# Attention and a gated FFN on one core: the last visits dealt anew, a step in halves in single banks, and X's transpositions no longer held

## The chip, the cores and the metric

The kernel runs on one core of a Trainium2 chip. The metric is device time in microseconds (us). Times before: a median of 419.72 us over three runs (419.26 to 419.96).

## The reference

```python
# q, k, v: (8, 12, 448, 64); w_gate, w_val: (768, 1536); w_out: (1536, 768)
scores = (q @ k.transpose(0, 1, 3, 2)) / sqrt(64)
attn = exp(scores - scores.max(-1)); attn = attn / attn.sum(-1)
x = (attn @ v).transpose(0, 2, 1, 3).reshape(8 * 448, 12 * 64)
g = x @ w_gate
out = (g * sigmoid(g) * (x @ w_val)) @ w_out          # (3584, 768), float32
```

Softmax attention over 8 batches and 12 heads is followed by a gated feed-forward network (FFN) over all 3584 tokens.

## The kernel before

The work is one hand-written order of instructions; the framework adds the waits, and each engine goes through its own list in order.

**Attention** goes by pairs of heads, 48 of them (6 in each batch). For a pair the queries and keys are copied by GpSimd (L240) and turned by a DMA transposition that SyncE (SP) issues (L244, tile `qkT`). TensorE makes scores `s` (L356, and L368 for leftover keys of two pairs together), ScalarE takes the exponential into `E` (L378), TensorE multiplies by V (L462, tile `acc`), and VectorE divides (L504, L505) into `xt`. `turn_x` turns `xt` into the matrix `X`, by DMA transpositions on SP: one of a pair's 384 long tokens (L550), and after each odd pair one of the 64 short tokens of two pairs (L556). `xt` has six buffers, so a pair reuses the buffer of the pair six before it. `X` holds two batches; the tiles come from a pool of two.

**The FFN of the first two X matrices** is done in between. A block has 384 or 512 tokens and 12 steps, one for each 128 columns of the hidden layer. A step makes a gate (`gp`, L610) and a value (`vp`, L610), each of six accumulating matmuls; ScalarE takes a tanh (`sg`), VectorE combines it with the gate (`t1`) and closes with the value (L696, into `hts`). It is run in one of three ways: whole (`run_fv`), as a pair of two steps (`run_pair`, 512 tokens wide, with the second step's value in halves), or in halves (`halves`, L660): gate halves of 256 tokens, two tanh (L670), two combinations (L675), two value halves, two closings (L696). A hidden block is then multiplied by `w_out`: by groups (`OutPair.wide`, L807, seven-product scheme, matmuls on L759), and, for the chunk of 128 tokens left over, by quarters of 192 columns (`plain_out`, L724, 12 matmuls on L732), scaled into `osb` by ScalarE (L742) or VectorE (L740); the fourth quarter also issues the chunk's two output DMAs.

**PSUM** is handed out by two pools: `ps_s`, three tiles of two banks, and `ps_f`, two single banks. Scores take `ps_s`, the products `acc` two of `ps_f`. A new tile waits for the readers of the tile three (or two) before it in its pool. `gate_small` tells a step to put its gate into `ps_f`; it is set in visits without products. `halves` doesn't look at it before the change.

**Visits.** The stretch around the change is a list of 33 visits (`VISITS`, L1108), each with up to three score tiles, up to one pair's products, and what its entry says: (block to begin, steps, groups, quarters, sums of VectorE). Every seventh visit is bare: it has scores but no products. They are the visits numbered 3, 10, 17, 24 and 31 from 0. In visit 24 the entry asks for two steps, which are run as a pair. A visit with one step and products runs it in halves (`lone`, L1297). Quarters stand in visits 25, 26, 27 and 29, groups in 28 and 31. `by_vector` (L1391) puts the scaling of the quarters on VectorE, except in visit 26. In the last visits, pairs 36 to 41 and on belong to the last X, whose buffer is that of the second X; as long as steps of the second X are left, their `turn_x` is held (`held`, L1345) and run after the last step (L1412).

After the visits come two phases of `Unit` (L929 onwards) and `OutPair` work for the last two X matrices, with sums of weights on GpSimd and sums of tokens on VectorE.

Of the kernel before, what the change touches and what calls it, by code (L numbers as in the profile page):

```python
# [10 lines left out]
FP32 = mybir.dt.float32  # L11
FP16 = mybir.dt.float16
# [5 lines left out]
NB = 2  # L18
# [10 lines left out]
NX = 6  # L29
# [36 lines left out]
def kernel(  # L66
# [10 lines left out]
    nc = tc.nc  # L77
    B, H, S, D = q.shape
# [4 lines left out]
    NCB = DM // 128  # L83
    NFB = DF // 128
    NHP = H // 2
# [5 lines left out]
    MQ = S - D  # L91
    KR = MQ // 128
# [18 lines left out]
    xp = ctx.enter_context(tc.tile_pool(name="xp", bufs=2))  # L111
# [10 lines left out]
    xts = consts.tile([128, NX, 8, D], FP16, name="xt")  # L122
# [35 lines left out]

    raw = {}
    qkT = {}  # L160
    X = {}

    def dummy(n, w=4):
        wp = ps_f.tile([128, 512], FP32, tag="f", name="wp")
# [362 lines left out]
        for c in range(NC):  # L527
            pv_chunk(pr, c)

    def turn_x(pr):  # L530
        b, hp = divmod(pr, NHP)
        kk, bb = divmod(b, NB)
        if kk not in X:
            X[kk] = xp.tile([128, NCB, NB * S], FP16, tag="X", name="X")
        dst = X[kk][:, hp, ts(bb, S)]
        xt = Xts[pr % NX]
        if pr < XPE:
            tp = accs[pr] if pr < FIRST else ps_f.tile([128, 512], FP32, tag="f", name="xtp")
            for j in range(3):
                nc.tensor.matmul(  # L540
                    tp[:, ts(j, 128)],
                    lhsT=xt[:, 2 * j : 2 * j + 2].rearrange("p h d -> p (h d)"),
                    rhs=ident[:],
                    start=True,
                    stop=True,
                )
            nc.vector.tensor_copy(dst[:, 0:MQ], tp[:, 0:MQ])
            return
        odd = pr % 2
        nc.sync.dma_start_transpose(  # L550
            dst[:, 0:MQ].rearrange("p (j q) -> p j q", j=KR),
            xt[:, 2 * odd : 2 * (KR + odd)].rearrange("p j d -> p (j d)"),
        )
        if odd:
            flat = xts[0:D, ts(pr % NX // 2, 2)].rearrange("p a j d -> p (a j d)")
            nc.sync.dma_start_transpose(X[kk][:, hp - 1 : hp + 1, ds(bb * S + MQ, D)], flat[:, ds(2 * KR * D, 4 * D)])  # L556

    def turn_rests(b):
        if b == 0:
# [15 lines left out]
    gate_small = [False]  # L575
# [23 lines left out]
    class Step:  # L599
# [60 lines left out]
        def halves(self):  # L660
            w = self.at[2] // 2
            parts = [ds(i * w, w) for i in range(2)]
            gs = ps_s.tile([128, 2, 512], FP32, tag="s", name="gp")
            self.sg = fp.tile([128, 512], FP32, tag="sg", name="sg")
            self.t1 = fp.tile([128, 512], FP32, tag="t1", name="t1")
            readers = []
            for i, part in enumerate(parts):
                g = gs[:, i, 0:w]
                apart(self.group("g", gs[:, i], range(NCB), (i * w, w)), *readers)
                tanh = nc.scalar.activation(self.sg[:, part], g, AF.Tanh, scale=0.5)  # L670
                for reader in readers[1:2]:
                    tc.declare_no_dep(tanh.ins, reader.ins, reason="another bank")
                readers.append(tanh)
                readers.append(
                    nc.vector.scalar_tensor_tensor(self.t1[:, part], self.sg[:, part], 1.0, g, ALU.add, ALU.mult)  # L675
                )
            while late_exp:
                late_exp.pop(0)()
            vps = [ps_f.tile([128, 512], FP32, tag="f", name="vp") for _ in parts]
            for i, vp in enumerate(vps):  # L680
                self.group("v", vp, range(NCB), (i * w, w))
            for i, vp in enumerate(vps):
                self.close(i * w, w, vp)
# [38 lines left out]
    by_vector = [False]  # L722
# [150 lines left out]
    NT = NB * S  # L873
# [152 lines left out]
    with tc.manual_schedule():  # L1026
# [52 lines left out]
        def add_block(i, visits):  # L1079
# [36 lines left out]
        ]  # L1116

        def token_sums(x, w, t, eng=nc.vector):
# [156 lines left out]
        base = min(x for x in adds if adds[x] == 2)  # L1275
        KL = B // NB - 1
        held = []
# [6 lines left out]
        for x, (chunks, todo) in enumerate(plan):  # L1284
# [9 lines left out]
            begins, nf, ng = VISITS[x - base][:3] if x >= base else (0, 0, 0)  # L1294
            if begins > 2:
                add_block(begins, 0)
            lone = nf == 1 and bool(todo)  # L1297
            behind = []
            for n, (pr, c) in enumerate(ordered if x else []):
                if ng and not todo:  # L1300
# [36 lines left out]
            for _, p0 in todo:  # L1337
                if split:
                    pv_split(p0)
                else:  # L1340
                    pv(p0)
                if p0 < XPE:
                    turns.append(p0)
                elif fvq and fvq[0].at[0] < p0 // NHP // NB - 1:
                    held.append(p0)  # L1345
                else:
                    turn_x(p0)
            for turn in ready:
# [9 lines left out]
            if 0 < base - x <= len(FIRST_STEPS):  # L1358
                n = FIRST_STEPS[x - base]
                gate_small[0] = bare  # L1360
                if n > 1:
                    run_pair()
                elif x < base - 1:
                    run_fv(True)
                    add_sum()
                else:
                    fvq.pop(0).halves()
                    add_sum()
            elif x < base:
                if bare and oq and not fvq:  # L1370
                    carry -= run_o()
                elif bare:
                    gate_small[0] = True
                out_small[0] = not fvq and bool(oq) and any(p0 >= QUAD for _, p0 in todo)
                extra = 2 * fvq[0].time if bare and len(chunks) == 3 and fvq and not fvq[0].at[1] else 0
                carry = run_budget(left() / (end - x) + carry + extra) - extra
            else:
                begins, nf, ng, no, ns = VISITS[x - base]
                gate_small[0] = bare
                out_small[0] = bool(no) and not bare  # L1380
                for _ in range(ng):
                    run_group(behind)
                if lone:
                    fvq.pop(0).halves()
                    add_sum()
                elif bare_next(x):
                    for _ in range(nf):
                        run_fv()
                else:
                    run_steps(nf)  # L1390
                by_vector[0] = x != len(VISITS) + base - 7  # L1391
                for _ in range(no):
                    run_o()
                    out_small[0] = True
                out_small[0] = False
                if begins == 2:
                    add_block(2, 0)
                ahead = {3: (x + 1, x + 2), 2: (), 1: ()}.get(len(VISITS) + base - x, (x + 1,))
                for p0 in [p for y in ahead for p in vcopies.get(y, [])]:
                    copy_v(p0)  # L1400
                add_sum(ns)
                if x == len(VISITS) + base - 6:
                    wsum_space(rfree[:, 2 * NK * S :], 3)
                    for t in qk16s:
                        wsum_space(t[:].rearrange("p t c h d -> p (t c h d)"), 2)
                    wsum_space(Eall, 4)
                    tsums6.extend(token_sums(X[KL - 1], S, t6))
# [2 lines left out]
            for u in {len(VISITS) + base - 6: range(2), len(VISITS) + base - 2: range(2, 3)}.get(x, []):  # L1410
                weight_sums(u)
            while held and not fvq:  # L1412
                turn_x(held.pop(0))
            while turns:
                turn_x(turns.pop(0))
        kept.extend(attp.tile([128, S], FP32, tag="qkT", name="kept", bufs=QB) for _ in range(4))
# [78 lines left out]
        p0 = NPAIR - 1  # L1495
# [13 lines left out]
        run_items(items)  # L1509

        apart_chunk = vfree[:, 6 * VE :].rearrange("p (f t) -> p f t", t=128)
        t7 = token_space(xp.tile([128, NCB, NT], FP16, tag="X", name="T")[:].rearrange("p a b -> p (a b)"), S)
        sums.clear()
        sums.extend(f for pair in pairs[1:] for f in pair.sums())
        sums.extend(token_sums(X[KL], S, t7))
# [41 lines left out]
```

## Time and profile before

| | |
|---|---|
| median of three runs | 419.72 us |
| profiled execution | 420.08 us |
| its span, first to last instruction | 418.3 us |
| granted TensorE clock in it | 1.000 |
| busy: PE / DVE / ACT / POOL | 412.2 / 273.7 / 248.9 / 225.4 us |
| visits 24 to 31 begin (us from the span's start) | 232.96, 238.95, 241.57, 244.40, 247.13, 255.75, 258.50, 260.17 |

In the profile PE is TensorE's matmuls, PEld its weight loads, DVE is VectorE, ACT ScalarE, POOL GpSimd, SPq the queue of SyncE. A timeline row gives start, duration, engine, line, operation, tiles and shapes; rows of equal instructions in a row are merged, with their count behind an x, and the duration is then from the first start to the last end. What an engine waited for stands in brackets. Matmuls are pipelined, so a matmul's row is longer than the spacing of starts.

### The profile page before, as it was taken

How to read it: one execution, taken by the hardware profiler on the slowest of the kernel's cores; microseconds unless marked ns; L12 is line 12 of the kernel's file. 1: busy time of each engine (PE TensorE's matmuls, PEld its weight loads, DVE VectorE, ACT ScalarE, POOL GpSimd, SP SyncE). 2: the span in 40 equal slices, each digit the busy share in tenths (PEclk: the TensorE clock that was granted, in tenths of full speed). 3: DMA queues.
4: the chain of work that ended last, by engine and by line, in shares of the span. 5: the costliest groups of instructions: out<-in, count | busy, mean ns of one | idle time of the engine just before them, and what ended most of it. 6: DMA issues, size and time to landing. Idle time of an engine off the chain costs nothing.

```text
span 418.3 us, 10870 instructions
## 1 busy us (share of the span) xinstructions
PE 412.2 (99%) x4346; PEld 260.4 (62%) x4346; DVE 273.7 (65%) x630; ACT 248.9 (59%) x387; POOL 225.4 (54%) x346
## 2 busy tenths in 40 slices
PE   8999999999999999999999999999999999999996
PEld 3666666655587786786767676555555655555664
DVE  4767562567786674579646578766757665757763
ACT  6975677656677675787656695655453345454121
POOL 8856534998898986398976814599800000000000
PEclk9999999999999999999999999999999999999999
DMA  9999999999999999999999935600000430000225
GB/s 135 192 200 200 200 177 195 129 166 205 196 142 179 153 194 172 154 158 151 167 159 171 102 62 106 186 18 0 2 0 2 121 107 0 2 0 0 76 79 150
DMA packets 108195, 50.29 MB, mean 120 GB/s; under 512 B 60400, under 2 KB 104816, under 8 KB 108144
## 3 DMA queue, kind: packets, MB, share of 16 engines
q0 software_dynamic: 46848, 24.56, 48.3%
q1 hardware_dynamic: 61024, 24.79, 34.7%
q8 instruction: 34, 0.56, 0.6%
q10 hardware_dynamic: 272, 0.25, 0.2%
q14 instruction: 17, 0.14, 0.1%
HBM read 49.55 MB, written 11.01 MB: 145 GB/s over the span
## 4 chain that ended last, share of the span: by engine, by line
PE 94%; DVE 2%; ACT 2%; issue 1%; ACTq 0%; DVEq 0%
PE gp L610 14%; PE un L929 12%; PE vp L610 12%; PE og L759 11%; PE ub L929 10%; PE ob L759 8%; PE acc L462 8%; PE s L356 5%; PE op L732 4%; PE s L393 2%; PE acc L426 2%; PE s L368 1%; PE tp L324 1%; PE wp L166 1%; ACT E L403 1%
## 5 line engine op out<-in xcount | busy, mean ns | idle before, releaser
L378 ACT ACTIVATE E<-s 128x896 f16<-128x896 f32 x126 | 107.4, 916 | 38.2 <-PE s L356 28.0
L610 PE MATMUL gp<-X,wg 128*128 128x256 f16 (+3 forms) x402 | 61.7, 300 | 0.0
L610 PE MATMUL vp<-X,wv 128*128 128x256 f16 (+3 forms) x402 | 58.6, 289 | 0.4 <-DVE xt L505 0.4
L240 POOL COPY qk<-qkraw 128x512 f16<-128x512 f16 x70 | 43.5, 668 | 22.8 <-DMA qkT<-qk 21.7
L180 POOL DMA_DIRECT2D vraw<-in_v_dram x72 | 44.1, 637 | 14.8 <-DMA wo<-in_moe_w_out_dram 8.0
L610 PEld LDWEIGHTS <-wv 128*128 128x128 f16 x444 | 41.6, 98 | 15.3 <-DVE xt L505 0.9
L610 PEld LDWEIGHTS <-wg 128*128 128x128 f16 x402 | 35.5, 98 | 15.8 <-issue 2.2
L180 POOL DMA_DIRECT2D qkraw<-in_k_dram x70 | 42.7, 630 | 4.9 <-DMA wo<-in_moe_w_out_dram 3.5
L403 ACT ACTIVATE E<-s 112x896 f16<-112x896 f32 x48 | 40.7, 918 | 7.5 <-PE s L393 7.5
L462 PEld LDWEIGHTS <-E 128*128 128x128 f16 (+2 forms) x1224 | 38.2, 98 | 8.5 <-issue 3.1
L462 PE MATMUL acc<-vo,E 128*128 128x65 f16 (+2 forms) x1224 | 42.1, 193 | 0.1
L759 PEld LDWEIGHTS <-hts 128*128 128x128 f16 x282 | 27.1, 98 | 17.0
L690 DVE SCALAR_TENSOR_TENSOR t<-sg,gp 128x384 f32<-128x384 f32 (+1 forms) x29 | 17.4, 614 | 24.3 <-ACT sg L637 24.3
L696 DVE SCALAR_TENSOR_TENSOR hts<-t,vp 128x256 f16<-128x256 f32 (+3 forms) x67 | 30.9, 461 | 3.5 <-PE vp L610 1.2
L505 DVE TENSOR_TENSOR xt<-acc,R 128x256 f16<-128x256 f32 x72 | 30.6, 425 | 2.5
L203 POOL DMA_DIRECT2D qkraw<-in_q_dram x44 | 30.2, 685 | 3.0 <-PE s L393 1.0
L356 PE MATMUL s<-qkT 64*64 64x448 f16 (+1 forms) x288 | 28.5, 352 | 0.0
L1002 ACT ACTIVATE silu<-un 128x448 f32<-128x448 f32 x24 | 13.1, 544 | 21.7 <-PE un L929 20.0
L759 PE MATMUL og<-wo,hts 128*128 128x384 f16 x132 | 25.4, 326 | 0.0
L986 DVE TENSOR_TENSOR un<-ub,kept 128x448 f32<-128x448 f32 x24 | 15.1, 631 | 15.6 <-ACT kept L983 10.2
L990 DVE TENSOR_TENSOR kept<-ub,kept 128x448 f32<-128x448 f32 x24 | 15.0, 625 | 13.2 <-PE ub L929 13.2
L979 ACT ACTIVATE ub<-un 128x448 f32<-128x448 f32 x24 | 12.7, 529 | 15.4 <-PE un L929 13.9
(213 smaller groups left out, 748.2 us busy)
## 6 DMA issues: line engine op xcount, KB each, us to landing
vraw<-in_v_dram POOLq DMA_DIRECT2D x72, 64.0 KB, 5.1
qkraw<-in_q_dram POOLq DMA_DIRECT2D x41, 112.0 KB, 4.7
qkraw<-in_k_dram POOLq DMA_DIRECT2D x68, 64.0 KB, 5.0
out_dram<-osb SPq DMA_DIRECT2D x7, 336.0 KB, 3.3
wg<-in_moe_w_gate_dram POOLq DMA_DIRECT2D x8, 288.0 KB, 9.5
wv<-in_moe_w_val_dram POOLq DMA_DIRECT2D x8, 288.0 KB, 10.0
wo<-in_moe_w_out_dram POOLq DMA_DIRECT2D x2, 1152.0 KB, 18.0
out_dram<-osb SPq DMA_DIRECT2D x7, 288.0 KB, 4.9
```

The costliest lines, as they stand in the source:

```text
L180: eng.dma_start(dst[ts(s, 64)], rows)
L203: nc.gpsimd.dma_start(dst, flat.rearrange("h (p c) d -> p h (c d)", c=NC))
L240: nc.gpsimd.tensor_copy(dst.rearrange("p c h d -> p h c d"), src)
L356: nc.tensor.matmul(s[ts(half, m), hx, 0:S].rearrange("p (c q) -> p c q", q=P), lhsT=t[ts(hx, 64), ds((c + low(pr, hx)) * 128 + half * m, m ...
L378: nc.scalar.activation(e, s[:, :, 0:S], AF.Exp, scale=sm_scale)
L403: nc.scalar.activation(e[:, :, 0:S], s[0:P, :, 0:S], AF.Exp, scale=sm_scale)
L462: nc.tensor.matmul(acc[ds(lo, m), ts((j + pr % 2) % (KR + 1), D + 1)], lhsT=e[rows, ds(hx * S + j * 128 + lo, m)], rhs=Vts[pr % NV][rows, ...
L505: nc.vector.tensor_tensor(xt[:, :, hx], a4[:, :, 0:D], r[:].unsqueeze(2).to_broadcast([128, KR + 1, D]), ALU.mult,)
L610: nc.tensor.matmul(dst[:, 0:w], lhsT=wslice(kind, self.fb, cb), rhs=X[kk][:, cb, ds(c0 + lo, w)], start=(cb == 0), stop=(cb == NCB - 1),)
L696: nc.vector.scalar_tensor_tensor(self.hts[:, self.fb, ds(lo, w)], self.t1[:, ds(lo, w)], 0.5 * HS, vp[:, 0:w], ALU.mult, ALU.mult)
L759: nc.tensor.matmul(dst, lhsT=lhs(n), rhs=rhs(n), start=first and n == 0, stop=n == NH - 1, skip_group_check=True)
L929: mm = nc.tensor.matmul(dst, lhsT=lhs[:, n], rhs=rhs[:, n], start=first and n == 0, stop=n == NK - 1, skip_group_check=True,)
```

## The change

- `VISITS`: visit 24 has one step in place of two, and visit 25 has one step in place of a quarter and the beginning of block 4, which moves to visit 26. Visit 30, which had scores and products only, gets a quarter. Quarters are now in visits 26, 27, 29 and 30. The sums of VectorE are 2, 2, 0, 2 in visits 26 to 29, where they were 1, 1, 2, 0, 2 in visits 25 to 29.
- `lone` no longer asks for products, so that the bare visit 24 runs its step in halves.
- `halves` in a bare visit takes two single banks of `ps_f` for its gate halves and one double tile of `ps_s` for its value halves, where it otherwise does the reverse.
- `by_vector` leaves the quarters of visits 26 and 27 to ScalarE.
- `turn_x` of the last X's pairs is run in the pair's own visit; only the transposition of the short tokens is held. The pool of X becomes two fixed buffers, and the last phase's sums of tokens lie in the one that is free.

```diff
+    Xbufs = [consts.tile([128, NCB, NB * S], FP16, name=f"X{i}") for i in range(2)]
+    X = [Xbufs[kk % 2] for kk in range(B // NB)]
...
-        if odd:
-            flat = xts[0:D, ts(pr % NX // 2, 2)].rearrange("p a j d -> p (a j d)")
-            nc.sync.dma_start_transpose(X[kk][:, hp - 1 : hp + 1, ds(bb * S + MQ, D)], flat[:, ds(2 * KR * D, 4 * D)])
+        if odd and with_rest:
+            turn_shorts(pr)
...
         def halves(self):
...
-            gs = ps_s.tile([128, 2, 512], FP32, tag="s", name="gp")
+            double = None if gate_small[0] else ps_s.tile([128, 2, 512], FP32, tag="s", name="gp")
...
-                g = gs[:, i, 0:w]
-                apart(self.group("g", gs[:, i], range(NCB), (i * w, w)), *readers)
+                bank = ps_f.tile([128, 512], FP32, tag="f", name="gp") if gate_small[0] else double[:, i]
+                g = bank[:, 0:w]
+                apart(self.group("g", bank, range(NCB), (i * w, w)), *readers if double is not None else ())
...
-            vps = [ps_f.tile([128, 512], FP32, tag="f", name="vp") for _ in parts]
+            if gate_small[0]:
+                gate_small[0] = False
+                double = ps_s.tile([128, 2, 512], FP32, tag="s", name="vp")
+                vps = [double[:, i] for i in range(2)]
+            else:
+                vps = [ps_f.tile([128, 512], FP32, tag="f", name="vp") for _ in parts]
...
-            (0, 0, 1, 0, 0), (0, 1, 0, 0, 0), (0, 1, 0, 0, 0), (0, 1, 0, 0, 0), (0, 2, 0, 0, 0),
-            (4, 0, 0, 1, 1), (0, 0, 0, 1, 1), (0, 0, 0, 1, 2), (0, 0, 1, 0, 0), (0, 0, 0, 1, 2),
-            (0, 0, 0, 0, 0), (0, 0, 1, 0, 0), (0, 0, 0, 0, 0),
+            (0, 0, 1, 0, 0), (0, 1, 0, 0, 0), (0, 1, 0, 0, 0), (0, 1, 0, 0, 0), (0, 1, 0, 0, 0),
+            (0, 1, 0, 0, 0), (4, 0, 0, 1, 2), (0, 0, 0, 1, 2), (0, 0, 1, 0, 0), (0, 0, 0, 1, 2),
+            (0, 0, 0, 1, 0), (0, 0, 1, 0, 0), (0, 0, 0, 0, 0),
...
-            lone = nf == 1 and bool(todo)
+            lone = nf == 1
...
-                    held.append(p0)
+                    turn_x(p0, False)
+                    if p0 % 2:
+                        held.append(p0)
...
-                by_vector[0] = x != len(VISITS) + base - 7
+                by_vector[0] = len(VISITS) + base - x not in (6, 7)
...
-                turn_x(held.pop(0))
+                turn_shorts(held.pop(0))
...
-        t7 = token_space(xp.tile([128, NCB, NT], FP16, tag="X", name="T")[:].rearrange("p a b -> p (a b)"), S)
+        t7 = token_space(Xbufs[KL % 2 ^ 1][:].rearrange("p a b -> p (a b)"), S)
```

More of the change, by code (lines that the diff above doesn't have):

```diff
@@ L110 @@
     attp = ctx.enter_context(tc.tile_pool(name="attp", bufs=4))
-    xp = ctx.enter_context(tc.tile_pool(name="xp", bufs=2))
     fp = ctx.enter_context(tc.tile_pool(name="fp", bufs=2))
@@ L160 @@
     qkT = {}
-    X = {}
+    Xbufs = [consts.tile([128, NCB, NB * S], FP16, name=f"X{i}") for i in range(2)]
+    X = [Xbufs[kk % 2] for kk in range(B // NB)]
     def dummy(n, w=4):
@@ L528, in pv, with turn_x @@
             pv_chunk(pr, c)
-    def turn_x(pr):
+    def turn_x(pr, with_rest=True):
         b, hp = divmod(pr, NHP)
         kk, bb = divmod(b, NB)
-        if kk not in X:
-            X[kk] = xp.tile([128, NCB, NB * S], FP16, tag="X", name="X")
         dst = X[kk][:, hp, ts(bb, S)]
@@ L553, in turn_x, with turn_shorts @@
         )
-        if odd:
-            flat = xts[0:D, ts(pr % NX // 2, 2)].rearrange("p a j d -> p (a j d)")
-            nc.sync.dma_start_transpose(X[kk][:, hp - 1 : hp + 1, ds(bb * S + MQ, D)], flat[:, ds(2 * KR * D, 4 * D)])
+        if odd and with_rest:
+            turn_shorts(pr)
+    def turn_shorts(pr):
+        b, hp = divmod(pr, NHP)
+        kk, bb = divmod(b, NB)
+        flat = xts[0:D, ts(pr % NX // 2, 2)].rearrange("p a j d -> p (a j d)")
+        nc.sync.dma_start_transpose(X[kk][:, hp - 1 : hp + 1, ds(bb * S + MQ, D)], flat[:, ds(2 * KR * D, 4 * D)])
     def turn_rests(b):
@@ L667, in halves @@
             for i, part in enumerate(parts):
-                g = gs[:, i, 0:w]
-                apart(self.group("g", gs[:, i], range(NCB), (i * w, w)), *readers)
+                bank = ps_f.tile([128, 512], FP32, tag="f", name="gp") if gate_small[0] else double[:, i]
+                g = bank[:, 0:w]
+                apart(self.group("g", bank, range(NCB), (i * w, w)), *readers if double is not None else ())
                 tanh = nc.scalar.activation(self.sg[:, part], g, AF.Tanh, scale=0.5)
-                for reader in readers[1:2]:
+                for reader in readers[1:2] if double is not None else []:
                     tc.declare_no_dep(tanh.ins, reader.ins, reason="another bank")
```

## The prediction

> **What bounds the kernel now.** I read the totals and the chain first, then TensorE's timeline over the stretch that the change reorders, then the same stretch on ScalarE and VectorE.
>
> ```profile
> span 418.3 us, 10870 instructions
> ...
> PE 412.2 (99%) x4346; PEld 260.4 (62%) x4346; DVE 273.7 (65%) x630; ACT 248.9 (59%) x387; POOL 225.4 (54%) x346
> ...
> PE 94%; DVE 2%; ACT 2%; issue 1%; ACTq 0%; DVEq 0%
> ```
>
> TensorE is busy for 412.2 of 418.3 us and makes 94% of the chain. So only two things can move the time: TensorE's own work, and short waits between its groups. Busy rows hide such waits, because a matmul's end is modelled. I therefore measure from start to start. The built order of the changed kernel differs on TensorE only from visit 24 of `VISITS` on (base row, 233.65 us); the phases after the visits hold the same matmuls in the same order.
>
> ```profile
> 230.24 1.47 PE L610 MATMUL gp<-X,wg 128*128 128x256 f16 x12
> 231.55 1.47 PE L610 MATMUL vp<-X,wv 128*128 128x256 f16 x12
> 232.96 0.38 PE L368 MATMUL s<-qkT 64*64 64x448 f16 x4
> ...
> 233.65 2.76 PE L610 MATMUL gp<-X,wg 128*128 128x512 f16 x12
> ...
> 238.95 0.74 PE L356 MATMUL s<-qkT 64*128 64x448 f16 x6
> 239.53 1.12 PE L462 MATMUL acc<-vo,E 64*128 64x65 f16 x32
> 240.49 1.15 PE L732 MATMUL op<-wo,hts 128*128 128x192 f16 x12
> 241.57 0.38 PE L368 MATMUL s<-qkT 64*64 64x448 f16 x4
> 241.94 0.57 PE L356 MATMUL s<-qkT 64*64 64x448 f16 x8
> 242.32 1.16 PE L462 MATMUL acc<-vo,E 64*64 64x65 f16 x40
> 243.31 1.15 PE L732 MATMUL op<-wo,hts 128*128 128x192 f16 x12
> 244.40 0.85 PE L356 MATMUL s<-qkT 64*128 64x448 f16 x6
> 245.07 1.14 PE L462 MATMUL acc<-vo,E 64*128 64x65 f16 x32
> ...
> 248.82 1.14 PE L759 MATMUL og<-wo,hts 128*128 128x384 f16 x6
> ```
>
> These are visit 23's last step (230.24), visit 24's pair of steps (233.65 to 238.95), visits 25, 26 and 27 with a quarter of an output product each (L732), and the start of visit 28's group (248.82). Scores before products take 0.58 us (238.95 to 239.53), and 0.67 in visit 27: the rest is a wait. Visit 26's scores take 0.75 where visit 24's took 0.69.
>
> ```profile
> 231.52 0.68 ACT L670 ACTIVATE sg<-gp 128x256 f32<-128x256 f32 x2
> 233.42 2.54 ACT L378 ACTIVATE E<-s 128x896 f16<-128x896 f32 x3 [1.22 <-PE s L368]
> 235.83 1.22 ACT L637 ACTIVATE sg<-gp 128x512 f32<-128x512 f32 x2
> 239.36 5.18 ACT L378 ACTIVATE E<-s 128x896 f16<-128x896 f32 x6 [2.31 <-PE s L356]
> 244.50 0.33 ACT L742 ACTIVATE osb<-op 128x192 f32<-128x192 f32 x1
> 244.86 2.54 ACT L378 ACTIVATE E<-s 128x896 f16<-128x896 f32 x3
> ```
>
> From 239.36 to about 247.4 ScalarE has no gap: visits with a quarter keep TensorE for 2.62 (238.95 to 241.57) and 2.83 us (to 244.40), and three exponentials take 2.54. This is the only place where TensorE waits for ScalarE here, and it waits little.
>
> **The change part by part.**
>
> *The pair becomes two visits in halves.* The pair took 5.30 us. One step in halves takes 1.31 + 1.41 = 2.72 (230.24 to 232.96), of which 0.10 is the turn from full to half-height tiles ahead of the scores. Visit 25's quarter had such a turn too (240.49 to 241.57 is 1.08, so 0.98 without it). Without any new wait, visit 26 would start at 233.65 + 2.72 + 0.58 + 0.96 + 2.72 = 240.63, where it now starts at 241.57. Taking the quarter's 0.98 away from that gives 240.59: the split itself costs 0.04 us.
>
> *Single banks: a new wait.* `halves` in visit 24 now puts its gate halves into the two single buffers of `ps_f`, and its value halves into a double tile of `ps_s`. That pool has three tiles. Visit 24 takes three for scores and the fourth for the values; visit 25's third score tile is then the same buffer as the values', so it must wait until VectorE has closed both halves (L696). The built order shows this wait on that matmul. The pair had the same buffer in use, but its last reader was through before visit 25's scores came: they take 0.58 now. The chain of releases goes over ScalarE and VectorE:
>
> ```profile
> 231.96 0.75 DVE L675 SCALAR_TENSOR_TENSOR t<-sg,gp 128x256 f32<-128x256 f32 x2 [0.69 <-ACT sg L670]
> 232.63 0.86 DVE L696 SCALAR_TENSOR_TENSOR hts<-t,vp 128x256 f16<-128x256 f32 x2
> ```
>
> ```profile
> 244.88 0.09 PEld L356 LDWEIGHTS <-qkT 64*128 64x128 f16 x1 [0.19 <-issue]
> ```
>
> Visit 24's three exponentials start at 233.42 as before, since nothing ahead of them changes, and the next ScalarE instruction starts at 235.83. That is the first tanh. The first L675 starts 0.44 later (231.52 to 231.96), the first L696 0.67 after that (231.96 to 232.63); four equal operations in 0.67 for two means 0.335 each, so the second L696 starts at 237.28 and ends 0.42 later (0.75 less 0.335), at 237.70. A score load came 0.05 after the ScalarE row that released it (244.50 + 0.33, then 244.88), so the third score starts at about 237.75. TensorE itself would be there at 233.65 + 2.72 + 2/3 of 0.58 = 236.76. **The new wait is 1.0 us.** Queued behind it on TensorE are that score tile, 32 products and the next 24 matmuls of the step; ScalarE waits for the score, but is still busy with the two exponentials ahead of it. Bounds: 0 if the scores find the buffer free, 0.65 if the first of the two closings were enough (0.335 less), 1.2 if each VectorE operation waited for the end of the row before it (3 times 0.08 more).
>
> [...]
>
> *Visits 25 to 28.* With the wait, visit 26 starts at 240.63 + 0.99 = 241.62, practically where it starts now. The exponentials of visit 25 are done by then, so the 0.06 of wait in visit 26's scores (0.75 against 0.69) can go; but the quarters of visits 26 and 27 are now both scaled on ScalarE (the new `by_vector`), 0.33 us each in the line of exponentials. Visit 26's exponentials start 0.46 after its scores (232.96 to 233.42), at 242.08, and end at 244.62; the scaling is then at 244.49 (2.41 after the first exponential, as 235.83 after 233.42) and the next exponentials at 244.85, against 244.86 now. So the group of visit 28 starts at 248.8 as before: the quarter taken out of visit 25 has paid for the wait.
>
> *The fourth quarter in visit 30.* It goes between the products and the group:
>
> ```profile
> 258.50 0.88 PE L356 MATMUL s<-qkT 64*128 64x448 f16 x6
> 259.20 1.13 PE L462 MATMUL acc<-vo,E 64*128 64x65 f16 x32
> 260.17 1.14 PE L759 MATMUL og<-wo,hts 128*128 128x384 f16 x6
> 261.15 1.14 PE L759 MATMUL og<-E,hts 128*128 128x384 f16 x6
> ```
>
> Products to group is 0.97 for 32 products and the group's first two products follow at 0.98: TensorE has no hole here that could take the quarter. Its 12 matmuls cost 0.98 in full. The scaling on VectorE and the quarter's two output DMAs go one visit later; the stores have until the end of the run.
>
> *X's transpositions.* Before, five transpositions of pairs 36 to 40 were held until the last value matmul of block 3 and stood on SP ahead of the next keys:
>
> ```profile
> 221.83 13.64 SPq L244 DMA_TRANSPOSE qkT<-qk  x3
> 239.05 2.48 SPq L550 DMA_TRANSPOSE X<-xt  x2
> 249.17 1.25 SPq L244 DMA_TRANSPOSE qkT<-qk  x1
> ```
>
> Now each goes out in its own visit, past three L244. A transposition on SP waits for VectorE's `xt`, and so the L244 behind it: pair 43's, issued at 221.83 now, would go out at about 228. The longest landing near it is 8.8 us:
>
> ```profile
> qkT<-qk SPq DMA_TRANSPOSE x1, 8.8
> ```
>
> It lands by 237, and its first reader is visit 26's first score at 241.6: 4 us to spare. GpSimd's copy for pair 46 waits for that landing, and the last V loads stand behind the copy; they are first read in visit 28. Cost 0, from below 0 (no wait for a key or X shows on TensorE now, so nothing to gain) to 1 us if the landing grew by 5. Two fixed X buffers in place of the pool change names and no order.
>
> **Sum.** 0.04 (split) + 0.99 (wait) - 0.98 (quarter out of visit 25) - 0.05 (waits of visits 26 to 28, which end where they do now) + 0.98 (quarter into visit 30) = +0.98 us. The profiled execution took 420.08 us, 1.78 around its span of 418.3; it would take 421.06. The median of the runs shown, 419.72, lies 0.36 below it: I predict **420.7 us**. A measurement of this kernel can tell about 0.2% (0.84 us) from no change.
>
> **The rivals.**
>
> *The wait does not bind* (not slower). Place: visit 25's third score. Price: 0 to 0.5 instead of 1.0. It decides if the closing of the second half ends before 236.8, which needs the chain of exponentials, tanh and four VectorE operations 0.9 us shorter than its rows. Against it: each row has been taken where nothing else held it. Then visits 26 to 28 start up to 0.98 earlier and the quarter in visit 30 takes it back: 419.7 to 420.2 us.
>
> *The quarter hides in visit 30.* ScalarE goes through visit 30's exponentials while TensorE begins the group. If the group waited for them, the quarter would cost nothing there: 419.7 with the new wait, 418.8 without. Against it: 0.97 and 0.98 from start to start at 260.17 and 261.15.
>
> *The early transpositions cost a second wait.* The short tokens of pairs 36 and 37 now stand on SP behind pair 46's keys and pair 40's X. Pair 42 reuses their buffer in visit 27, where VectorE writes `xt` at about 246:
>
> ```profile
> 245.88 0.18 DVE L504 RECIPROCAL R<-acc 128x4 f32<-128x4 f32 x1 [0.87 <-PE acc L462]
> ```
>
> By SP's spacing of 1.25 us they go out at about 242.5 to 243 and land around 245 to 246. A later landing holds VectorE's `xt`, and visit 28's products behind it once it exceeds about 0.8 us: 421 to 422 us. [...]
>
> **How the numbers follow.** Forecast 0.50 (420.2 to 421.2); the wait doesn't bind 0.24; the quarter hides 0.11, of which 0.08 without the wait; early transpositions cost 0.15. The range must take in the unbound wait and most of the last case: 419.4 to 421.6. Faster by over 0.2% (below 418.9): 0.08. Slower by over 0.2% (above 420.56): 0.36 of the forecast's half and 0.13 of the last case, 0.49. Within: 0.43.
>
> **What would show it.** Right: a third L356 pair of visit 25 about 1 us after the second, behind the second L696; visit 28's group at 248.8 from the span's start; L732 ahead of visit 30's group and that group 1.0 us later. Wrong: scores of visit 25 in 0.58 us, or a group of visit 31 that starts where it does now. VectorE's `xt` of visit 27 waiting for a DMA would show the last rival.

## The result, and the profile after

The changed kernel took a median of **420.94 us** (420.31 to 421.13, nine runs) against 419.72 for the kernel before (419.26 to 420.36, nine runs, taken beside it). The ratio is 1.0023, 95% interval 1.0014 to 1.0033: slower by 0.14 to 0.33%. I had predicted 420.7, or +0.98 us; the medians lie 1.22 apart. The profiled execution of the changed kernel took 420.91 us, its span is 419.1.

Lines from 550 on have moved: the steps' matmuls L610 are L613 now, the tanh L670 is L674, the combinations L675 are L679, the closings L696 are L705, the quarters L732 are L741, a quarter's scaling L740 or L742 is L749 or L751, the groups L759 are L768, VectorE's sums L593 to L596 are L596 to L599, GpSimd's sums of weights L892 to L895 are L901 to L904, and the units L929 are L938.

The first view is TensorE's timeline after the change (start, duration, engine, line, tiles, shapes, count, wait).

```profile
232.69 0.38 PE L368 MATMUL s<-qkT 64*64 64x448 f16 x4
...
236.11 0.55 PE L356 MATMUL s<-qkT 64*128 64x448 f16 x4
237.47 0.36 PE L356 MATMUL s<-qkT 64*128 64x448 f16 x2 [0.80 <-DVE hts L705]
237.65 1.13 PE L462 MATMUL acc<-vo,E 64*128 64x65 f16 x32
...
241.34 0.38 PE L368 MATMUL s<-qkT 64*64 64x448 f16 x4
...
247.53 1.32 PE L462 MATMUL acc<-vo,E 64*64 64x65 f16 x40
248.69 1.14 PE L768 MATMUL og<-wo,hts 128*128 128x384 f16 x6
...
258.36 0.88 PE L356 MATMUL s<-qkT 64*128 64x448 f16 x6
259.06 1.13 PE L462 MATMUL acc<-vo,E 64*128 64x65 f16 x32
260.03 1.15 PE L741 MATMUL op<-wo,hts 128*128 128x192 f16 x12
261.02 1.14 PE L768 MATMUL og<-wo,hts 128*128 128x384 f16 x6
...
271.32 0.73 PE L938 MATMUL un<-X,wg 128*128 128x448 f16 x3
```

Visit 25's first four score matmuls start at 236.11, the third pair at 237.47 behind L705, where the four matmuls ahead of it would have let it start at about 236.49 (two thirds of the 0.58 that six take): a wait of 0.98. The quarter L741 stands between visit 30's products and the group, which comes 0.99 later for it (260.03 to 261.02).

The spans of the two executions differ ahead of the change too: visit 24 begins at 232.69 here and at 232.96 before. So I count from visit 24's first score. Before, the units began here:

```profile
270.47 0.73 PE L929 MATMUL un<-X,wg 128*128 128x448 f16 x3
```

| us from visit 24's first score | before | after | added in this stretch |
|---|---|---|---|
| visit 26 | 8.61 | 8.65 | +0.04 |
| visit 28's group | 15.86 | 16.00 | +0.10 |
| visit 31's group | 27.21 | 28.33 | +0.98 |
| units | 37.51 | 38.63 | 0.00 |

The trace gives +1.12 from visit 24 on, close to the 1.22 of the medians; the two profiled executions as wholes are 0.83 apart (420.08 and 420.91), because this one comes to visit 24 0.27 earlier. The chain that makes the wait, on ScalarE and on VectorE, after the change:

```profile
233.15 2.54 ACT L378 ACTIVATE E<-s 128x896 f16<-128x896 f32 x3 [1.21 <-PE s L368]
235.56 0.68 ACT L674 ACTIVATE sg<-gp 128x256 f32<-128x256 f32 x2
```

```profile
236.00 0.75 DVE L679 SCALAR_TENSOR_TENSOR t<-sg,gp 128x256 f32<-128x256 f32 x2 [2.57 <-ACT sg L674]
236.67 0.75 DVE L705 SCALAR_TENSOR_TENSOR hts<-t,vp 128x256 f16<-128x256 f32 x2
```

Tanh 2.41 after the first exponential, the combination 0.44 later, the first closing 0.67 later, the second ending at 237.42, the score 0.05 behind it: the spacings of the prediction, one by one.

The 0.10 between visits 26 and 28 was not forecast (I had them 0.05 shorter). Here VectorE's timeline after the change, and GpSimd's beside it:

```profile
243.85 0.92 DVE L221 COPY vo<-vraw 128x512 f16<-128x512 f16 x1
244.69 1.26 DVE L596 TENSOR_TENSOR qkraw<-hts 128x768 f16<-128x768 f16 x1
245.99 0.56 DVE L597 TENSOR_TENSOR hts<-hts 128x768 f16<-128x768 f16 x1
...
247.22 0.42 DVE L505 TENSOR_TENSOR xt<-acc,R 128x256 f16<-128x256 f32 x1
```

```profile
244.58 0.95 POOL L901 TENSOR_TENSOR qk<-wv 128x384 f16<-128x384 f16 x1
246.11 1.20 POOL L902 TENSOR_TENSOR qk<-qk,wv 128x384 f16<-128x384 f16 x1 [0.57 <-DMA qkT<-qk]
```

And the same two engines before the change:

```profile
242.34 0.55 DVE L593 TENSOR_TENSOR qkraw<-hts 128x768 f16<-128x768 f16 x1
...
244.25 0.28 DVE L221 COPY vo<-vraw 128x512 f16<-128x512 f16 x1
```

```profile
241.35 0.91 POOL L892 TENSOR_TENSOR qk<-wv 128x384 f16<-128x384 f16 x1
253.23 0.91 POOL L893 TENSOR_TENSOR qk<-qk,wv 128x384 f16<-128x384 f16 x1 [10.97 <-DMA qkT<-qk]
```

Two operations of VectorE on fp16 data take 0.92 and 1.26 us where they took 0.28 and 0.55, while GpSimd makes its sums of weights. Before, GpSimd stood idle from 242.3 to 253.2, waiting for a DMA; now its last key copy, its V loads and its sums lie 3 us later, right beside VectorE's sums of tokens. This became a second theory: not the DMAs of the early transpositions cost time, but the work of GpSimd that they push to another place. VectorE's last division of visit 27 then ends at 247.64, after visit 28's products have begun. TensorE's loads for these products name that division:

```profile
247.70 1.03 PEld L462 LDWEIGHTS <-E 64*64 64x64 f16 x39 [0.25 <-DVE xt L505]
```

So the products take 1.16 to the group (247.53 to 248.69) in place of 0.99 (247.83 to 248.82).

### The profile page after: what moved, and what is told of

Its sections match the earlier page's. It is cut to its first block, busy times and chain, and to the rows that moved or that the text cites. A ratio compares the mean times of both kernels' runs of the same rounds, so it can differ in the third digit from the quotient of the medians.

```text
span 419.1 us, 10916 instructions
## 1 busy us (share of the span) xinstructions
PE 411.8 (98%) x4364; PEld 262.1 (63%) x4364; DVE 273.2 (65%) x632; ACT 249.3 (59%) x390; POOL 226.7 (54%) x346
## 4 chain that ended last, share of the span: by engine, by line
PE 95%; DVE 2%; ACT 1%; DMA 1%; issue 0%; SPq 0%; DVEq 0%; ACTq 0%
PE gp L613 14%; PE un L938 12%; PE vp L613 12%; PE og L768 11%; PE ub L938 10%; PE acc L462 8%; PE ob L768 8%; PE s L356 6%; PE op L741 4%; PE s L393 2%; PE acc L426 2%; PE s L368 1%; PE tp L324 1%; DMA rk<-in_k_dram 1%; ACT E L403 1%; PE acc L434 1%
## 5 line engine op out<-in xcount | busy, mean ns | idle before, releaser
L613 PE MATMUL gp<-X,wg 128*128 128x256 f16 (+3 forms) x414 | 61.9, 296 | 0.0
L613 PE MATMUL vp<-X,wv 128*128 128x256 f16 (+3 forms) x414 | 59.3, 287 | 0.0
L240 POOL COPY qk<-qkraw 128x512 f16<-128x512 f16 x70 | 44.5, 684 | 24.1 <-DMA qkT<-qk 23.5
L613 PEld LDWEIGHTS <-wv 128*128 128x128 f16 x450 | 42.3, 98 | 13.7
L613 PEld LDWEIGHTS <-wg 128*128 128x128 f16 x414 | 36.6, 98 | 14.9 <-issue 2.2
L768 PEld LDWEIGHTS <-hts 128*128 128x128 f16 x282 | 27.1, 98 | 17.0
L705 DVE SCALAR_TENSOR_TENSOR hts<-t,vp 128x256 f16<-128x256 f32 (+3 forms) x69 | 31.3, 455 | 3.3 <-PE vp L613 0.9
L505 DVE TENSOR_TENSOR xt<-acc,R 128x256 f16<-128x256 f32 x72 | 30.6, 425 | 2.5
L699 DVE SCALAR_TENSOR_TENSOR t<-sg,gp 128x384 f32<-128x384 f32 (+1 forms) x27 | 16.1, 608 | 21.2 <-ACT sg L640 21.2
L768 PE MATMUL og<-wo,hts 128*128 128x384 f16 x132 | 25.4, 326 | 0.0
L679 DVE SCALAR_TENSOR_TENSOR t<-sg,gp 128x256 f32<-128x256 f32 (+1 forms) x42 | 15.7, 394 | 10.7 <-ACT sg L674 9.2
```

Source lines behind the costliest of these rows:

```text
L240: nc.gpsimd.tensor_copy(dst.rearrange("p c h d -> p h c d"), src)
L505: nc.vector.tensor_tensor(xt[:, :, hx], a4[:, :, 0:D], r[:].unsqueeze(2).to_broadcast([128, KR + 1, D]), ALU.mult,)
L613: nc.tensor.matmul(dst[:, 0:w], lhsT=wslice(kind, self.fb, cb), rhs=X[kk][:, cb, ds(c0 + lo, w)], start=(cb == 0), stop=(cb == NCB - 1),)
L705: nc.vector.scalar_tensor_tensor(self.hts[:, self.fb, ds(lo, w)], self.t1[:, ds(lo, w)], 0.5 * HS, vp[:, 0:w], ALU.mult, ALU.mult)
L768: nc.tensor.matmul(dst, lhsT=lhs(n), rhs=rhs(n), start=first and n == 0, stop=n == NH - 1, skip_group_check=True)
```

## The experiments

Positions are from visit 24's first score again; for the changed kernel they are 8.65 (visit 26), 16.00 (visit 28's group), 28.33 (visit 31's group), 38.63 (units). Every ratio is to the kernel before, run on the same chip (its medians there 419.61 to 419.69). Except for X's transpositions alone and the two runs that took over 422 us, the intervals overlap that of the changed kernel (1.0014 to 1.0033). So what a run says of one part is read from the positions in one execution of it, not from its median.

**The new wait: more of it.** One more VectorE operation stands between the combinations and the closings.

```diff
+                nc.vector.scalar_tensor_tensor(
+                    self.sg[:, parts[1]], self.t1[:, parts[1]], 1.0, self.t1[:, parts[1]], ALU.mult, ALU.mult
+                )
```

> The changed kernel with one more VectorE operation of the same size (a square written to a tile that nobody reads afterwards) between the combinations and the closings of visit 24. My theory (the wait of visit 25's third score is this chain): the wait grows by one spacing, 0.33 us, to 1.3 us, and the run by 0.3 us to 421.2 us. Rival (TensorE's third score is held by something else, a load of keys or ScalarE): the score comes where it did, 420.9 us.

Measured 421.08 us (ratio 1.0033, 1.0022 to 1.0044). VectorE, then TensorE:

```profile
235.78 0.75 DVE L679 SCALAR_TENSOR_TENSOR t<-sg,gp 128x256 f32<-128x256 f32 x2 [2.26 <-ACT sg L674]
236.57 0.42 DVE L687 SCALAR_TENSOR_TENSOR sg<-t 128x256 f32<-128x256 f32 x1
236.91 0.74 DVE L708 SCALAR_TENSOR_TENSOR hts<-t,vp 128x256 f16<-128x256 f32 x2
```

```profile
237.71 0.36 PE L356 MATMUL s<-qkT 64*128 64x448 f16 x2 [1.26 <-DVE hts L708]
```

The wait is 1.43 and visit 26 stands at 9.10, 0.45 later; the units stand at 38.89, 0.26 later, because visits 26 to 28 took only 7.16 here (7.35 in the changed kernel). The time from combination to closing grew by 0.46 (0.67 to 1.13), more than the 0.335 of one operation, because the added one reads what the operation right before it wrote and starts only after its end (235.78 + 0.75, then 236.57; in the same run L505, which reads what L504 wrote, starts at 238.92 after 238.70 + 0.18). So every bit of VectorE's chain is on TensorE's path here.

**The new wait: without single banks.** Visit 24's step takes its tiles as any other step in halves.

```diff
-                gate_small[0] = bare
+                gate_small[0] = bare and not lone
```

> The changed kernel without its single banks: visit 24's halves put the gate into a double tile and the values into single banks, as other visits do. My theory: the gate now waits for the first exponential (about 0.7 us from 233.4 on) and the third score for nothing, since its buffer is free after the second combination; visit 26 starts 0.25 us earlier than in the changed kernel, 420.7 us. Rival (the single banks are what costs): the run returns to about 420.0 us.

Measured 420.80 us (1.0029, 1.0013 to 1.0044). TensorE:

```profile
234.19 1.47 PE L613 MATMUL gp<-X,wg 128*128 128x256 f16 x12 [0.67 <-ACT E L378]
...
236.90 0.74 PE L356 MATMUL s<-qkT 64*128 64x448 f16 x6
```

The third score no longer waits; the gate does, for an exponential to free its `ps_s` tile. Visit 26 stands at 8.43, so single banks lose 0.22 against that. The change trades one wait of the same pool for another.

**The new wait: the third exponential behind the tanh**, once alone and once with eight `xt` buffers for six.

```diff
-                late = late or n == 2 and lone and not fvq[0].at[1]
+                late = late or n == 2 and lone and (not todo or not fvq[0].at[1])
```

> The changed kernel with the third exponential of visit 24 behind the two tanh in ScalarE's list, so that the chain tanh, combinations, closings starts one exponential (0.81 us from start to start) earlier; TensorE's list is untouched. My theory (visit 25's third score waits for the second closing, 0.98 us in the changed kernel's trace): the wait shrinks to 0.1 to 0.3 us, and the run is about 0.8 us shorter than the changed kernel, 420.1 us. Rival (the closing is only the last of several reasons, or the cost lies in the quarter or the transpositions): the third score comes no earlier or the gain is eaten by visit 28, 420.6 to 421.0 us.

> The third exponential of visit 24 behind the two tanh, as in the run before (late_third), and eight buffers for xt in place of six, so that pair 42 no longer reuses the buffer from which pair 36's short tokens are transposed. In late_third's trace visit 25's wait fell from 0.98 to 0.53 less the usual spacing, but VectorE's xt in visit 27 then waited 1.06 us for something that isn't an engine, and visit 28's products 0.78. My theory (that is the DMA of the short tokens): both waits go, visit 28's group starts about 15.2 us after visit 24 (16.0 in the changed kernel, 16.5 in late_third), and the run takes 420.1 us. Rival (VectorE waits for its own sums beside GpSimd): xt waits as before, 420.4 us.

Measured 420.44 us (1.0017, 1.0007 to 1.0027) and 420.73 (1.0028, 1.0016 to 1.0040). Both fall short of the 420.1 that I expected. VectorE in the first of them:

```profile
235.84 0.75 DVE L705 SCALAR_TENSOR_TENSOR hts<-t,vp 128x256 f16<-128x256 f32 x2 [0.28 <-PE vp L613]
...
243.24 1.27 DVE L596 TENSOR_TENSOR qkraw<-hts 128x768 f16<-128x768 f16 x1
244.54 1.15 DVE L597 TENSOR_TENSOR hts<-hts 128x768 f16<-128x768 f16 x1
...
246.84 0.42 DVE L505 TENSOR_TENSOR xt<-acc,R 128x256 f16<-128x256 f32 x1 [1.06 <-issue]
```

The wait falls from 0.98 to 0.53 only (third score at 236.65, wanted at 236.12), and visit 26 stands at 8.20: with the tanh early, the closings wait for TensorE's own value halves. Visit 27's `xt` then stands still for 1.06 us; the profile names no cause, but the buffer is the one whose short tokens SP sent out at 241.5. With eight buffers that gap is gone. The third rival's mechanism exists, then, but in these two runs other costs follow: visits 26 to 28 took 8.34 and 7.45.

**The new wait: filled.** Visit 25's third score is issued behind its products.

```diff
+                if x == len(VISITS) + base - 8 and n == 2:
+                    third.append((pr, c, small))
+                    continue
...
+            for unit in third:
+                qk(*unit)
```

> The changed kernel, but visit 25's third score and its exponential are issued behind that visit's 32 products instead of ahead of them. If the new wait of 0.98 us is all that the change costs between visits 24 and 26, the products fill it: the third score waits for nothing, visit 26 starts about 7.67 us after visit 24's first score (8.65 in the changed kernel), the units about 37.7 (38.63), and the time is about 420.0 us. Rival (VectorE's fp16 operations beside GpSimd's sums and the short tokens' transposition give the time back before visit 28, as when the third exponential was late): group 28 no earlier than 15.6 and the time 420.4 to 420.7.

Measured **420.14 us** (1.0004, 0.9992 to 1.0016): no difference from the kernel before can be told. TensorE, its loads, and VectorE:

```profile
235.83 0.55 PE L356 MATMUL s<-qkT 64*128 64x448 f16 x4
236.22 1.42 PE L462 MATMUL acc<-vo,E 64*128 64x65 f16 x32
237.57 0.36 PE L356 MATMUL s<-qkT 64*128 64x448 f16 x2
237.87 1.49 PE L613 MATMUL gp<-X,wg 128*128 128x256 f16 x12
```

```profile
236.03 0.25 PEld L462 LDWEIGHTS <-E 64*128 64x128 f16 x2
236.53 0.99 PEld L462 LDWEIGHTS <-E 64*128 64x128 f16 x30 [0.24 <-issue]
```

```profile
235.72 0.75 DVE L679 SCALAR_TENSOR_TENSOR t<-sg,gp 128x256 f32<-128x256 f32 x2 [2.32 <-ACT sg L674]
```

The third score waits for nothing now, yet visit 26 stands at 8.18, not at 7.67. The products take 1.35 to the next row where 32 take 0.96: after two of them TensorE stops until 236.53, just behind the second combination (235.72 + 0.75 = 236.47). The gate halves lie in the two single banks that the products need, so the products follow L679. That is read from the times and the buffers, not tested by a run of its own. Another 0.12 is the score pair standing alone (0.30 where it took 0.18). From there on it goes as before: visit 28's group at 15.34, visit 31's at 27.67, units at 37.97, which is 0.46 behind the kernel before; the medians differ by 0.45.

**The fourth quarter**, cut from twelve products to one in all the chunk's last quarters.

```diff
+        nfb = 1 if w < OH and m0 + w == DM else NFB
-        for fb in range(NFB):
+        for fb in range(nfb):
...
-                stop=fb == NFB - 1,
+                stop=fb == nfb - 1,
```

> The changed kernel with the fourth quarter, in visit 30, cut from 12 matmuls to 1 (192 columns of one chunk of 128 tokens are then not the full product); its scaling and its two DMAs stay. My theory (the quarter costs TensorE its full 0.98 us there): 0.9 us shorter than the changed kernel, 420.0 us. Rival (the group of visit 31 waits for ScalarE's exponentials and hides the quarter): less than 0.3 us shorter, 420.6 to 420.9 us.

Measured 420.28 us (1.0015, 1.0006 to 1.0024); visit 31's group at 27.87, 0.46 earlier and not 0.9. TensorE in visit 30:

```profile
258.74 1.13 PE L462 MATMUL acc<-vo,E 64*128 64x65 f16 x32
259.70 0.25 PE L742 MATMUL op<-wo,hts 128*128 128x192 f16 x1
260.27 1.14 PE L769 MATMUL og<-wo,hts 128*128 128x384 f16 x6 [0.32 <-ACT E L378]
```

A quarter takes a tile of the pool as well as time: the group's tile is then the one of visit 30's second score, and waits for its exponential. The twelve products hide that wait. So the quarter's price is read best from the changed kernel itself: from visit 30's first score to the group 2.66 us (258.36 to 261.02), before 1.67 (258.50 to 260.17).

**X's transpositions: alone, and undone.** Once the kernel before gets only this part of the change; once the changed kernel holds whole transpositions again.

```diff
-                    turn_x(p0, False)
-                    if p0 % 2:
-                        held.append(p0)
+                    held.append(p0)
...
-                turn_shorts(held.pop(0))
+                turn_x(held.pop(0))
```

> The kernel before with the X part of the change alone: two fixed X buffers, long tokens turned in their own visit, only the short tokens held; visits, halves and quarters as before. My theory: 419.7 us, no difference, and 7.25 us from visit 26 to the group of visit 28. Rival (GpSimd's weight sums move beside VectorE's work and lengthen visits 26 to 28, or a held-up short transposition makes VectorE wait): 419.8 to 420.2 us with 7.35 to 7.5 us for these visits.

> The changed kernel with whole transpositions of X held again, as before the change. My theory as predicted (the early transpositions cost nothing): 420.9 us, visits 26 to 28 take 7.35 us as in the changed kernel. Rival, formed from the changed kernel's trace, where VectorE's sum L596 took 1.26 us in visit 26 against 0.55 before and visit 28's products 1.16 against 0.99: the earlier keys let GpSimd's weight sums run beside VectorE's copies and sums, and this makes visits 26 to 28 longer. Then holding again gives 7.15 to 7.25 us for visits 26 to 28 and 420.7 us.

Alone they gave 419.94 us (1.0003, 0.9994 to 1.0012), units at 37.72, 0.21 later than before; held again 420.95 (1.0029, 1.0017 to 1.0040), units at 38.72. The medians alone say only that the part is worth less than can be told; the traces say where it goes. Visits 26 to 28 take 7.42 with the part alone (7.25 before) and 7.16 with all held (7.35 in the changed kernel). VectorE with the part alone, and with all held:

```profile
241.84 1.27 DVE L596 TENSOR_TENSOR qkraw<-hts 128x768 f16<-128x768 f16 x1
...
244.82 1.26 DVE L597 TENSOR_TENSOR hts<-hts 128x768 f16<-128x768 f16 x1
```

```profile
243.45 0.55 DVE L596 TENSOR_TENSOR qkraw<-hts 128x768 f16<-128x768 f16 x1
```

With all held GpSimd's sums are over at 241.9. But the gain of 0.19 is given back in visit 30, whose scores take 0.99 to the products in place of 0.70: VectorE meets GpSimd's sums there (its copy L221 takes 0.79 us), and its scaling of visit 29's quarter, which frees the third score's tile, ends only at 258.32 (in the first of the runs on GpSimd's sums, below, TensorE's row at this place names that scaling). So by these two traces the part as a whole costs the changed kernel nothing: undone, it saves 0.19 in visits 26 to 28 and costs 0.29 in visit 30, and the units come 0.09 later, not earlier.

**Eight `xt` buffers alone** (`NX = 8` for 6).

> The changed kernel with eight buffers for xt in place of six, nothing else. My theory: the changed kernel's xt in visit 27 started right after VectorE's sum (246.46, no gap), so the short tokens were not what it waited for there: no change, 420.9 us, group of visit 28 at 16.0 us after visit 24. Rival (in most executions the short tokens land later than in the profiled one and cost part of the 1.2 us): 420.3 to 420.7 us.

Measured 421.17 us (1.0035, 1.0022 to 1.0048): no gain. In this execution L596 and L597 took 1.26 and 1.17 and visit 28's products waited 0.34 us for `xt`; visits 26 to 28 took 7.76. In the changed kernel, VectorE's `xt` doesn't wait for a DMA (its row at 246.67 in visit 27 shows no wait), so buffers have nothing to give.

**GpSimd's sums out of the way.** Three runs. In the first two I laid the first four sums into E's space and left them where they were issued, in visit 27.

```diff
+                    wsum_space(Eall, 4)
                     wsum_space(rfree[:, 2 * NK * S :], 3)
...
-                    wsum_space(Eall, 4)
```

> As the run before, and GpSimd's first four sums of weights are laid into the space of E, which comes free only after the last exponentials, so that they do not run beside VectorE's sums of tokens in visits 26 to 28. If the overlap is what lengthens visits 26 to 28 (7.35 us in the changed kernel), they take about 7.16 here, the units start at 37.4 to 37.5 and the time is 419.5 to 419.8, no slower than the kernel before. Rival (the overlap does nothing to the path, or the later sums are late for the last phase): no earlier than the run before, 420.0 or more.

> The changed kernel with GpSimd's first four sums of weights laid into the space of E and nothing else altered. If GpSimd's sums slow VectorE's fp16 operations beside them, the 768-wide sum of VectorE in visit 26 takes 0.55 us (1.26 in the changed kernel), visits 26 to 28 take 7.15 to 7.2 (7.35), and the time is about 420.75. Rival (VectorE's operations are long for another reason, such as the transpositions' DMA traffic): 1.2 us and 7.35 as before, 420.9.

Measured 422.23 us (1.0057, 1.0039 to 1.0076) and 422.60 (1.0063, 1.0043 to 1.0084). These two change the computation: later exponentials are written over the sums, so the last phase multiplies by other weights. As times they failed, since the sums now stood between two exponentials of the same space, and visit 28's products waited for GpSimd. But they show VectorE on both sides of GpSimd's start (244.82), in the first of them:

```profile
243.21 0.55 DVE L596 TENSOR_TENSOR qkraw<-hts 128x768 f16<-128x768 f16 x1
...
247.65 1.26 DVE L598 TENSOR_TENSOR hsum<-hts 128x768 f16<-128x768 f16 x1
248.95 1.15 DVE L599 TENSOR_TENSOR qkraw<-hts,hsum 128x768 f16<-128x768 f16 x1
```

The third run keeps this layout and issues the sums after visit 31, so that they wait for visit 30's products. It computes what the changed kernel computes.

```diff
-            for u in {len(VISITS) + base - 6: range(2), len(VISITS) + base - 2: range(2, 3)}.get(x, []):
+            for u in {len(VISITS) + base - 2: range(3)}.get(x, []):
```

> The changed kernel, but GpSimd's sums of weights are issued after visit 31, the first four of them into E's space, so that none of them starts before the products of visit 30 have read E there (about 260 us from the span's start; they run from 240.9 on in the changed kernel). Nothing else is altered. If GpSimd's sums slow VectorE's fp16 operations beside them and that is what lengthens visits 26 to 28: the first 768-wide sum of VectorE takes 0.55 us (1.26), visits 26 to 28 take 7.15 to 7.2 (7.35), the units start at about 38.45 after visit 24 (38.63) and the time is about 420.75. Rival (the length has another cause, or the sums are then late for the units): 7.35 and 420.9 or more.

Measured 420.85 us (1.0031, 1.0021 to 1.0041). GpSimd, VectorE, then TensorE:

```profile
259.18 0.91 POOL L901 TENSOR_TENSOR E<-wg 128x384 f16<-128x384 f16 x1 [19.05 <-PE acc L462]
```

```profile
243.59 0.55 DVE L596 TENSOR_TENSOR qkraw<-hts 128x768 f16<-128x768 f16 x1
...
245.79 0.42 DVE L505 TENSOR_TENSOR xt<-acc,R 128x256 f16<-128x256 f32 x1 [0.49 <-DMA X<-xt]
```

```profile
240.88 0.38 PE L368 MATMUL s<-qkT 64*64 64x448 f16 x4
...
247.04 1.16 PE L462 MATMUL acc<-vo,E 64*64 64x65 f16 x40
248.03 1.14 PE L768 MATMUL og<-wo,hts 128*128 128x384 f16 x6
```

In the trace all three numbers came as expected: L596 0.55, visits 26 to 28 7.15, units at 38.44; from products to group it is 0.99 again. SP sends out the short tokens 9.61 after visit 24's first score (241.84), as in the changed kernel (9.62), so it is GpSimd's sums that lengthen L596 and not the DMAs. The times can't show a part this small: the median is 0.09 below the changed kernel's, but the ratio is above its ratio (1.0031 against 1.0023). Note the row at 245.79: with VectorE early again, `xt` waits 0.49 for the transposition of the short tokens, and TensorE doesn't notice.

A slow sum costs time only where it reaches TensorE. With the third score behind the products L596 took 1.26 as well, yet visits 26 to 28 took 7.16. Visit 27's last division ended 6.02 after visit 26's first score there, ahead of visit 28's products at 6.16; in the changed kernel it ended at 6.30.

## Why the prediction was right

**The split** (+0.04): visit 26 begins 0.04 later than before, with the wait and the quarter gone from visit 25 cancelling. Right as a whole.

**The new wait** (+0.99): right in place, chain and size (0.98). A longer chain lengthens it one for one (0.46 more of chain, 0.45 more of wait), and other tiles remove it. The case with only the first closing, 0.65, and the case with each operation waiting for the one before, 1.2, are both out. From start to start the rows have 0.335 again, and 0.455 where an operation reads what the one before it wrote (the row of 236.57).

**The quarter out of visit 25** (-0.98) and **into visit 30** (+0.98): right, 0.99 in visit 30 by the rows. My reason held for the changed kernel, and one thing I didn't see: the quarter also shifts the pool, and would put a wait of about 0.5 ahead of the group if it were shorter (one product to the group took 0.57, where a twelfth of 0.99 is 0.08).

**Visits 26 to 28** (-0.05): this failed by 0.15. "The group of visit 28 starts at 248.8 as before" came out as 16.00 after visit 24's first score against 15.86. Without GpSimd beside VectorE the forecast is met (7.15, forecast 248.8 less 241.62, 7.18). With it they take 7.35 here, and 7.16 where VectorE is through in time.

**X's transpositions** ("cost 0", with 1 us as the upper bound): visits 26 to 28 lose about 0.2 by them, within the bounds, but by a way I had not listed. In the kernel before, the part alone costs 0.21 by the trace; in the changed kernel it saves 0.29 in visit 30, so there the sum of 0 holds by two effects that I didn't see, which is luck. I followed the chain SP, GpSimd's copy, V loads, to its first reader in visit 28 and found 4 us to spare; I didn't follow it one step further, to the sums of weights behind the loads. SP's times were nearly right: pair 43's keys went out at 228.06 (forecast 228), the short tokens at 242.31 (forecast 242.5 to 243).

**The rivals.** *The wait does not bind*: out. *The quarter hides*: out. *Early transpositions cost a second wait*: in the changed kernel out, as VectorE's slower sums bring it to `xt` after the DMA (the row at 246.67 shows no wait). Where VectorE comes to it earlier the wait appears: 0.27 and 0.49 in the second and third run on GpSimd's sums, without cost, 1.06 with the third exponential late and 1.58 in the first run on GpSimd's sums, where products waited. My point of decision, about 0.8 us, lies between them. The profile names the DMA in all but the case of 1.06.

**What stays open.** The trace assigns +1.12 and the medians say 1.22 with an interval of about 0.8 across, so the 0.20 that visits 26 to 28 lose beside GpSimd's sums (7.35 against 7.15) is shown in traces, not in medians. In the stretch where GpSimd runs beside VectorE single executions differ by some tenths: the profiled execution of the kernel with the third exponential late took 421.05 us, 0.6 above its median, and its units stand at 39.17, later than the changed kernel's. No version here beat the kernel before; the best version of the changed kernel, with the third score behind the products, can't be told from it in time and is 0.46 longer by the trace. The change could hardly win: it moves one quarter from a place where it cost 0.98 to another where it costs 0.98, and pays for whatever waits it makes.

## What to carry to other kernels

When work is moved on an engine that never stops, nothing is gained by the moving itself (0.98 us out of visit 25, 0.99 into visit 30): ask which wait goes, and if none does, count the new ones. In this kernel a tile of two banks is released as a whole, so putting two results into one makes the next user wait for the later of them (visit 25's third score started 0.05 behind the second closing, with 0.98 of wait); follow that release over every engine, row by row from start to start. And when a DMA is issued earlier or later, follow the engines behind it to the end of their lists: what is pushed may meet another engine's work there (L596 took 1.26 us beside GpSimd's sums, 0.55 apart from them), though nobody waits for it. Whether that costs time depends on how much room the slowed engine has before the next one wants its result.

## What the runs showed of the hardware

In these runs VectorE's sums and copies of fp16 data took longer beside GpSimd's sums: in the changed kernel 1.26 us for a sum of 128x768 (L596) and 0.92 for a copy of 128x512 (L221), against 0.55 and 0.28 in the kernel before. Not each one grew so much: in the kernel before, copies that began beside GpSimd's sums took 0.36 and 0.47 (at 239.40 and 241.95). VectorE's divisions of `acc` (L505), which lies in PSUM, kept their 0.42, also beside L902 (246.11 to 247.31). In the changed kernel L596 began at 244.69 within L901 (244.58 to 245.53) and ended at 245.95, 0.42 after it, and L597, begun at 245.99 while GpSimd stood waiting, took 0.56. By what means GpSimd's sums lengthen VectorE's operations, no run shows.
